# fp32 loads on the SP queue and head preparation one group ahead, in a fused attention and FFN kernel

## The chip, the cores and the metric

The kernel runs on one core of one Trainium2 chip. The metric is the device time in microseconds (us), the median over several executions. A single execution can be profiled; its span is the time from the first to the last instruction, about 2 us less than the timed value.

The engines are written as the profile writes them: PE is TensorE, PEld its weight loads, DVE VectorE, ACT ScalarE, POOL GpSimd, SP SyncE. L121 is line 121 of that run's kernel; the changed kernel's lines are shifted by one to seven against those of the kernel before. A timeline line gives the start and the length in us, the engine, the line, the operation, the result<-its inputs, their shapes and the number of instructions, and in brackets how long the engine had been idle before it and what ended that.

## The reference, cut to what matters

```python
# q, k, v: 8 batches, 12 heads, 448 positions, head size 64, float32
q_n = q / (norm(q, axis=-1) + 1e-06)
k_n = k / (norm(k, axis=-1) + 1e-06)
attn = softmax(q_n @ k_n.T / tau) @ v
x = attn.transpose(0, 2, 1, 3).reshape(3584, 768)
a, b = x @ w1, x @ w2              # 768 -> 1024
out = ((a * b) @ w3) @ w_out       # 1024 -> 1024 -> 768
```

The kernel computes the product w3 @ w_out once (it calls it w34) and then out = (a * b) @ w34.

## The kernel before

The 96 heads are 48 pairs, and the pairs are 16 groups g of three. The main loop has 101 steps t. A pair takes two of them, so a group takes six, s = 0 to 5. In a step PE does two score products of one pair, the attention-times-v product (av) of the pair before, and two pieces of "filler": in the beginning the preparation of w34, from t = 14 on the FFN groups a, b and out of the batches whose attention is done. In every odd step PE also transposes the normalised q and k of the next pair.

A pair has to be prepared before its transposes: squares of q and k, their sums, a root, a reciprocal, and a multiply. This is the schedule of that work in the kernel before:

```python
    def prep_step(s, g):
        if s == 0 and g + 3 < NG:
            load_qk(g + 3)
        ...                                   # v of g + 2, its copy
        n = g + 2
        if n < NG:
            if s < GP:                        # GP = 3
                prep_sq(n, s, nc.gpsimd)      # squares on POOL
            if 1 <= s <= GP:
                prep_sum(n, s - 1)            # sums on DVE
            if s == GP + 1:
                prep_rn(n)                    # root (DVE, ACT), reciprocal (DVE)
        n = g + 1
        if n < NG and s >= GP:
            prep_scale(n, s - GP, nc.gpsimd)  # multiplies on POOL
```

So while group g is computed, group g+2 gets its squares to reciprocals, and group g+1 its multiplies. The order in a step is fixed by the program, engine by engine:

```python
    for t in range(2 * NP + 5):
        ...
        scores(pp, half)
        ...
        if half == 1 and pp + 1 < NP:
            tr(pp + 1)                        # transposes of the next pair
        ...
        filler()
        av(pp - 1, half)
        filler()
        prep_step(s, g)
```

All loads are casting loads (fp32 in memory, bf16 in SBUF) in POOL's queue, q and k in three buffers:

```python
    load_qk(0, 0, 2)
    load_qk(0, 2, GH)
    load_v(0)
    load_w(w3_sb, moe_w3)
    load_qk(1)
    load_w(wo_sb, moe_w_out)
    load_v(1)
    load_w(w1_sb, moe_w1)
    load_w(w2_sb, moe_w2)
    load_qk(2)
```

## Time and profile before

| kernel before | value |
|---|---|
| timed, median of 3 | 451.41 us (451.37 to 452.33) |
| span of the profiled run | 448.6 us, mean granted PE clock 0.988 |
| busy share PE / DVE / ACT / POOL | 87% / 62% / 48% / 57% |
| scores of t = 4 start at | 58.32 us |
| scores of t = 14 start at | 101.18 us |
| from there to the end | 347.4 us |

The two start times are read from the timeline: they are the score products that open these steps. The step t = 14 is the first with FFN work, and from there the body is the same chain of PE work in both kernels. So a kernel's span can be split at that instant into a start and a body. The prediction below shows the lines themselves. In the body PE is busy without a gap, and only in the start does it wait.

### The profile page before, as it was taken

The page shows a single profiled execution, that of the slowest core. Times are in us where ns is not written, and L with a number is a line of the kernel's source. Part 1 is how long each engine was busy: PE and PEld are TensorE (multiplying, and loading weights), DVE is VectorE, ACT ScalarE, POOL GpSimd, SP SyncE. Part 2 cuts the span into 40 slices and gives each one's busy share as a digit, 9 for nine tenths or more (in the row PEclk, how much of TensorE's full clock was granted, in tenths as well). Part 3 has the DMA queues.
Part 4 walks back from the last instruction along what each step waited for, and adds up shares of the span by engine and source line. Part 5 has one row for each costly group of instructions (what it writes and reads, how often), then busy time and mean ns, then how long its engine had stood idle before and what let it go on. Part 6 is the DMA issues. An engine that isn't in the chain of part 4 may idle for free.

```text
span 448.6 us, 9291 instructions
## 1 busy us (share of the span) xinstructions
PE 389.9 (87%) x3904; PEld 228.6 (51%) x3904; DVE 276.6 (62%) x605; ACT 215.8 (48%) x319; POOL 253.6 (57%) x265
## 2 busy tenths in 40 slices
PE   0030579989999999999998999999989999999996
PEld 0010456655555555655565556555655565556553
DVE  2055397877685868576858685768576855564321
ACT  1011334345655565556556655565566555554121
POOL 9148499986767676757676767576747150000000
PEclk9999879999999999999999999999999999999999
DMA  8999916715062706280718071907130011001003
GB/s 108 208 207 213 200 16 91 94 15 81 4 92 77 122 4 91 82 154 2 94 72 129 0 94 72 164 1 94 72 67 1 1 72 72 1 1 72 35 1 140
DMA packets 40776, 34.92 MB, mean 78 GB/s; under 512 B 1312, under 2 KB 34592, under 8 KB 40736
## 3 DMA queue, kind: packets, MB, share of 16 engines
q0 software_dynamic: 36704, 23.33, 37.1%
q1 hardware_dynamic: 4032, 11.01, 6.4%
q8 instruction: 30, 0.49, 0.5%
q14 instruction: 10, 0.08, 0.1%
HBM read 46.66 MB, written 11.01 MB: 129 GB/s over the span
## 4 chain that ended last, share of the span: by engine, by line
PE 80%; DMA 10%; DVE 7%; POOL 1%; issue 0%; ACT 0%; POOLq 0%; ACTq 0%
PE ps_o L220 16%; PE ps_b L220 16%; PE ps_a L220 16%; PE ps_av L193 10%; PE sc L177 10%; DMA raw<-in_k_dram 7%; PE ps_tr L159 5%; PE ps_w L220 4%; DMA w_sb<-in_moe_w_dram 4%; PE ps_tb L211 3%; DVE ss L128 2%; DVE qT L166 1%; DVE w3t_sb L227 1%; DVE osd L202 1%; POOL raw L98 1%; DVE rt L136 1%
## 5 line engine op out<-in xcount | busy, mean ns | idle before, releaser
L184 ACT ACTIVATE expT<-sc 112x896 bf16<-112x896 f32 x192 | 165.4, 914 | 99.6 <-PE sc L177 99.6
L121 POOL TENSOR_TENSOR sq<-raw 112x512 bf16<-112x512 bf16 x90 | 91.5, 1041 | 55.3 <-DVE ss L128 47.7
L146 POOL TENSOR_TENSOR nrm<-raw,rn 112x512 bf16<-112x512 bf16 x96 | 96.8, 1044 | 44.4 <-DVE rn L140 44.4
L220 PEld LDWEIGHTS <-w_sb 128*128 128x128 bf16 x768 | 68.6, 97 | 49.9
L220 PE MATMUL ps_a<-xT,w_sb 128*128 128x448 bf16 x384 | 83.8, 352 | 0.6 <-DVE xT L214 0.3
L220 PE MATMUL ps_b<-xT,w_sb 128*128 128x448 bf16 x384 | 83.1, 352 | 0.0
L220 PE MATMUL ps_o<-w_sb,abT 128*128 128x384 bf16 x448 | 80.8, 326 | 0.0
L177 PE MATMUL sc<-qT,kT 64*112 64x448 bf16 x384 | 58.2, 380 | 23.7 <-DVE qT L166 16.3
L193 PEld LDWEIGHTS <-expT 112*128 112x128 bf16 x1536 | 62.9, 99 | 15.8 <-issue 1.7
L128 DVE TENSOR_REDUCE ss<-sq 112x8 f32<-112x512 bf16 x96 | 61.3, 677 | 14.6 <-POOL sq L121 14.6
L193 PE MATMUL ps_av<-v_sb,expT 112*128 112x65 bf16 x1536 | 66.2, 195 | 0.0
L258 DVE TENSOR_TENSOR abT<-a_sb,ps_b 128x448 bf16<-128x448 bf16 x64 | 39.7, 621 | 37.1 <-PE ps_b L220 34.4
L166 DVE COPY qT<-ps_tr 128x448 bf16<-128x448 bf16 x48 | 55.2, 1150 | 0.0
L220 PEld LDWEIGHTS <-abT 128*128 128x128 bf16 x448 | 41.0, 98 | 23.3 <-issue 0.3
L159 PE MATMUL ps_tr<-ident,nrm 112*128 112x112 bf16 x384 | 28.3, 217 | 23.6 <-POOL nrm L146 23.6
L177 PEld LDWEIGHTS <-kT 64*112 64x112 bf16 x384 | 17.9, 127 | 56.5 <-issue 24.0
L202 DVE TENSOR_TENSOR osd<-ps_av,rs 128x256 bf16<-128x256 f32 x96 | 40.7, 424 | 3.8
L247 ACT CAST a_sb<-ps_a 128x448 bf16<-128x448 f32 x64 | 34.1, 534 | 17.5 <-PE ps_a L220 15.5
L159 PEld LDWEIGHTS <-nrm 112*128 112x128 bf16 x384 | 20.1, 99 | 40.0 <-POOL nrm L146 24.7
L275 ACT COPY out_sb<-ps_o 128x384 f32<-128x384 f32 x28 | 13.4, 479 | 54.4 <-PE ps_o L220 54.4
L165 DVE COPY kT<-ps_tr 128x448 bf16<-128x448 bf16 x48 | 17.7, 368 | 30.8 <-PE ps_tr L159 30.8
L201 DVE RECIPROCAL rs<-ps_av 128x4 f32<-128x4 f32 x96 | 17.7, 185 | 25.7 <-PE ps_av L193 25.7
(30 smaller groups left out, 222.9 us busy)
## 6 DMA issues: line engine op xcount, KB each, us to landing
out_dram<-out_sb SPq DMA_DIRECT2D x28, 384.0 KB, 2.3
vraw<-in_v_dram POOLq DMA_DIRECT2D x16, 336.0 KB, 7.3
raw<-in_q_dram POOLq DMA_DIRECT2D x15, 336.0 KB, 5.0
raw<-in_k_dram POOLq DMA_DIRECT2D x15, 336.0 KB, 6.8
w_sb<-in_moe_w_dram POOLq DMA_DIRECT2D x2, 1536.0 KB, 35.1
w_sb<-in_moe_w_dram POOLq DMA_DIRECT2D x1, 2048.0 KB, 15.7
wo_sb<-in_moe_w_out_dram POOLq DMA_DIRECT2D x1, 1536.0 KB, 24.3
raw<-in_q_dram POOLq DMA_DIRECT2D x1, 224.0 KB, 4.8
```

Source lines behind the costliest of these rows:

```text
L121: eng.tensor_mul(s.rearrange("p h j d -> p (h j d)"), x, x)
L128: nc.vector.reduce_sum(sss[g][:, t, 2 * i:2 * i + 2, :], sqs.pop((g, i, t)), axis=AX.X)
L146: eng.tensor_mul(nrms[g][:, i, t].rearrange("p j h d -> p h j d"), raws[g][:, t, 2 * i:2 * i + 2], rns[g][:, t, 2 * i:2 * i + 2].to_broadc ...
L159: nc.tensor.transpose(ps[:, t, j * P:(j + 1) * P], n[:, i, t, j].rearrange("p h d -> p (h d)"), ident[:P, :P])
L166: nc.vector.tensor_copy(qts[pp].rearrange("p (t j) -> p j t", j=NJ), ps[:, 0, :S].rearrange("p (j t) -> p j t", j=NJ))
L177: nc.tensor.matmul(sc[:P, hh, :S], kts[pp][64 * hh:64 * hh + 64, c * P:(c + 1) * P], qts[pp][64 * hh:64 * hh + 64, :], start=True, stop=True)
L184: nc.scalar.activation(exps[pp][:, c], sc[:P, :, :S], ACT.Exp, scale=1.0 / float(tau))
L193: nc.tensor.matmul(ps[:, m, :], exps[pp][:, c, hh, q0:q0 + 128], vt[:, 2 * i + hh, c, :], start=(c == 0), stop=(c == NJ - 1))
L202: nc.vector.tensor_mul(osds[pp][:, :, hh, :], ps[:, :, :D], rs.to_broadcast([128, NJ, D]))
L220: nc.tensor.matmul(o, l, r, start=(i == 0), stop=(i == len(pairs) - 1))
L247: nc.scalar.copy(a_sbs[b, fo], ps[:, :S])
L258: nc.vector.tensor_mul(abts[b // 2][:, fo, c0:c0 + S], a_sbs.pop((b, fo)), ps[:, :S])
```

## The change

The intent is a shorter start. q, k and v come as fp32 through the SP queue, with no cast on the way, so that they no longer stand behind two megabytes of w3 in one queue (in the kernel before, the issue of group 2's k waits 9.27 us for a weight load, and its q and k take 39.1 and 30.8 us from issue to landing). The weights stay in POOL's queue, in other pieces and later. And the preparation runs one group ahead instead of two, in smaller steps. That needs two buffers of q, k and of the normalised heads instead of three, and it takes group 2's preparation out of the start. To make room, the squares get four buffers instead of six, v one instead of two, and w3 shares the buffer of the product a * b (abT). The filler at the start comes later (from the third pair on) and joins each w3 transpose with the product that needs it.

The core of the diff, with cuts:

```diff
-    raw_pool = ctx.enter_context(tc.tile_pool(name="raw", bufs=3))
+    raw_pool = ctx.enter_context(tc.tile_pool(name="raw", bufs=2))
-    nrm_pool = ctx.enter_context(tc.tile_pool(name="nrm", bufs=3))
+    nrm_pool = ctx.enter_context(tc.tile_pool(name="nrm", bufs=2))
...
-            raws[g] = raw_pool.tile([P, 2, GH, NJ, D], BF16, tag="raw", name="raw")
+            raws[g] = raw_pool.tile([P, 2, GH, NJ, D], FP32, tag="raw", name="raw")
...
-            nc.gpsimd.dma_start(
+            nc.sync.dma_start(
...
+    prep_sq(0, 0, DVE, (0,))
+    prep_sq(0, 0, POOL, (1,))
+    load_w(wo_sb, moe_w_out, 0, KO2)
+    load_w(w3_sb, moe_w3, 0, 2)
+    load_w(w3_sb, moe_w3, 2, 4)
...
     def prep_step(s, g):
+        n = g + 1
+        if s == 0:
+            prep_scale(g, 2, (POOL, POOL))
+        if s == 1 and g + 2 < NG:
+            load_qk(g + 2)
...
+        if s < GP:
+            prep_sq(n, s, POOL)
...
+        if 1 <= s <= GP:
+            prep_sum(n, s - 1)
+        if s == GP:
+            prep_root(n)
+        if s == GP + 1:
+            prep_rn(n)
+            prep_scale(n, 0, (POOL, POOL))
+        if s == GP + 2:
+            prep_scale(n, 1, (POOL, POOL))
...
-    fill += [w3t_group(fo) for fo in range(KO2)]
-    fill += [w34_group(fo, mh) for fo in range(KO2) for mh in range(2)]
+    for fo in range(KO2):
+        fill.append(lambda fo=fo: (w3t_group(fo)(), w34_group(fo, 0)()))
+        fill.append(w34_group(fo, 1))
```

`prep_root` is the root alone, `prep_rn` now only the reciprocal. The lists `(DVE, POOL)` give the engine for q and for k.

More of the change, by code (lines that the diff above doesn't have):

```diff
@@ L55 @@
     wpool = ctx.enter_context(tc.tile_pool(name="wpool", bufs=1))
-    raw_pool = ctx.enter_context(tc.tile_pool(name="raw", bufs=3))
-    sq_pool = ctx.enter_context(tc.tile_pool(name="sq", bufs=3))
+    raw_pool = ctx.enter_context(tc.tile_pool(name="raw", bufs=2))
+    sq_pool = ctx.enter_context(tc.tile_pool(name="sq", bufs=4))
     st_pool = ctx.enter_context(tc.tile_pool(name="st", bufs=3))
-    nrm_pool = ctx.enter_context(tc.tile_pool(name="nrm", bufs=3))
+    nrm_pool = ctx.enter_context(tc.tile_pool(name="nrm", bufs=2))
     head_pool = ctx.enter_context(tc.tile_pool(name="head", bufs=2))
@@ L62 @@
     xpool = ctx.enter_context(tc.tile_pool(name="xt", bufs=2))
-    ab_pool = ctx.enter_context(tc.tile_pool(name="ab", bufs=2))
+    ab_pool = ctx.enter_context(tc.tile_pool(name="ab", bufs=1))
     opool = ctx.enter_context(tc.tile_pool(name="opool", bufs=3))
@@ L71 @@
     nc.scalar.preload_act_table_set("natural_log_exp_and_others")
-    ident = const.tile([128, 128], BF16)
-    make_identity(nc, ident)
     w1_sb = wpool.tile([128, KO1, DF], BF16, name="w1_sb")
@@ L78 @@
     w34_sb = wpool.tile([128, KO2, DM], BF16, name="w34_sb")
-    w3_sb = wpool.tile([128, KO2, DF], BF16, name="w3_sb")
     w3t_sb = wpool.tile([128, KO2, DF], BF16, name="w3t_sb")
     wo_sb = wpool.tile([128, KO2, DM], BF16, name="wo_sb")
+    w3_sb = ab_pool.tile([128, KO2, DF], BF16, tag="big", name="w3_sb")
     NV = 3
     v_tiles = [wpool.tile([P, GH, NJ, D + 1], BF16, name=f"v{i}_sb") for i in range(NV)]
-    for t in v_tiles:
-        nc.gpsimd.memset(t[:, :, :, D:D + 1], 1.0)
-    raws, vraws, nrms, rns, sss = {}, {}, {}, {}, {}
+    raws, vraws, nrms, rns, sss, sqs = {}, {}, {}, {}, {}, {}
     def heads_of(g):
@@ L103, in load_v, with spread_v, load_w, prep_sq @@
         b, hb = heads_of(g)
-        vraws[g] = raw_pool.tile([P, GH, NJ, D], BF16, tag="vraw", name="vraw", bufs=2)
-        nc.gpsimd.dma_start(
+        vraws[g] = raw_pool.tile([P, GH, NJ, D], FP32, tag="vraw", name="vraw", bufs=1)
+        nc.sync.dma_start(
             out=vraws[g], in_=v[b, hb:hb + GH].rearrange("h (p j) d -> p h j d", j=NJ))
-    def spread_v(g):
-        nc.gpsimd.tensor_copy(v_tiles[g % NV][:, :, :, :D], vraws.pop(g))
-    def load_w(t, w):
-        nc.gpsimd.dma_start(out=t, in_=w.rearrange("(ko p) n -> p ko n", p=128))
-    sqs = {}
-    def prep_sq(g, i, eng):
+    def spread_v(g, eng):
+        eng.tensor_copy(v_tiles[g % NV][:, :, :, :D], vraws.pop(g))
+    def load_w(t, w, k0, k1):
+        nc.gpsimd.dma_start(out=t[:, k0:k1], in_=w.rearrange("(ko p) n -> p ko n", p=128)[:, k0:k1])
+    def prep_sq(g, i, eng, ts=(0, 1)):
         r = raws[g]
-        for t in range(2):
-            s = sq_pool.tile([P, 2, NJ, D], BF16, tag="sq", name="sq", bufs=6)
+        for t in ts:
+            s = sq_pool.tile([P, 2, NJ, D], BF16, tag="sq", name="sq")
             x = r[:, t, 2 * i:2 * i + 2].rearrange("p h j d -> p (h j d)")
@@ L122, in prep_sq, with prep_sum, rn_views, prep_root @@
             sqs[g, i, t] = s
-    def prep_sum(g, i):
+    def prep_sum(g, i, ts=(0, 1)):
         if g not in sss:
             sss[g] = st_pool.tile([P, 2, GH, NJ], FP32, tag="ss", name="ss")
-        for t in range(2):
+        for t in ts:
             nc.vector.reduce_sum(sss[g][:, t, 2 * i:2 * i + 2, :], sqs.pop((g, i, t)), axis=AX.X)
-    def prep_rn(g, i0=0, i1=GP):
+    def rn_views(g, i0, i1):
         sl = slice(2 * i0, 2 * i1)
+        return rns[g, "t"][:, :, sl, :], sss[g][:, :, sl, :], rns[g][:, :, sl, :, 0]
+    def prep_root(g, i0=0, i1=GP):
         if g not in rns:
             rns[g] = st_pool.tile([P, 2, GH, NJ, 1], FP32, tag="rn", name="rn")
-            rns[g, 't'] = st_pool.tile([P, 2, GH, NJ], FP32, tag="rt", name="rt")
-        t, ss = rns[g, 't'][:, :, sl, :], sss[g][:, :, sl, :]
+            rns[g, "t"] = st_pool.tile([P, 2, GH, NJ], FP32, tag="rt", name="rt")
+        t, ss, _ = rn_views(g, i0, i1)
         nc.vector.tensor_scalar_max(t, ss, TINY)
@@ L138, in prep_rn, with prep_scale @@
         nc.scalar.activation(t, t, ACT.Exp, scale=0.5)
+    def prep_rn(g, i0=0, i1=GP):
+        t, _, rn = rn_views(g, i0, i1)
         nc.vector.tensor_scalar_add(t, t, NORM_EPS)
-        nc.vector.reciprocal(rns[g][:, :, sl, :, 0], t)
-    def prep_scale(g, i, eng):
+        nc.vector.reciprocal(rn, t)
+    def prep_scale(g, i, engs):
         if g not in nrms:
@@ L145, in prep_scale @@
         for t in range(2):
-            eng.tensor_mul(
+            engs[t].tensor_mul(
                 nrms[g][:, i, t].rearrange("p j h d -> p h j d"),
@@ L252, in f @@
             if b % 2 == 0 and fo == 0:
-                abts[b // 2] = ab_pool.tile([128, KO2, 2 * S], BF16, tag="abT", name="abT", bufs=1)
+                abts[b // 2] = ab_pool.tile([128, KO2, 2 * S], BF16, tag="big", name="abT")
             ps = psM.tile([128, 512], FP32, tag="pm", name="ps_b")
@@ L293, in filler @@
                 fill.pop(0)()
+    DVE, POOL = nc.vector, nc.gpsimd
     load_qk(0, 0, 2)
@@ L297 @@
     load_v(0)
-    load_w(w3_sb, moe_w3)
     load_qk(1)
-    load_w(wo_sb, moe_w_out)
-    load_v(1)
-    load_w(w1_sb, moe_w1)
-    load_w(w2_sb, moe_w2)
-    load_qk(2)
-    prep_sq(0, 0, nc.vector)
+    ident = const.tile([128, 128], BF16)
+    make_identity(nc, ident)
+    POOL.memset(v_tiles[0][:, :, :, D:D + 1], 1.0)
+    prep_sq(0, 0, DVE, (0,))
[3 more added lines that the diff above has]
+    load_w(w3_sb, moe_w3, 2, 4)
     prep_sum(0, 0)
+    prep_root(0, 0, 1)
@@ L308 @@
+    prep_sq(0, 1, DVE)
     prep_rn(0, 0, 1)
-    prep_scale(0, 0, nc.gpsimd)
+    prep_scale(0, 0, (DVE, POOL))
     tr(0)
-    spread_v(0)
-    prep_sq(0, 1, nc.vector)
-    prep_sq(0, 2, nc.vector)
     prep_sum(0, 1)
-    prep_sum(0, 2)
-    prep_rn(0, 1, GP)
-    prep_scale(0, 1, nc.gpsimd)
-    prep_scale(0, 2, nc.gpsimd)
-    def prep_step(s, g):
-        if s == 0 and g + 3 < NG:
-            load_qk(g + 3)
-        if s == 0 and g + 2 < NG:
-            load_v(g + 2)
-        if s == GP - 1 and g + 1 < NG:
-            spread_v(g + 1)
-        n = g + 2
-        if n < NG:
-            if s < GP:
-                prep_sq(n, s, nc.gpsimd)
-            if 1 <= s <= GP:
-                prep_sum(n, s - 1)
-            if s == GP + 1:
-                prep_rn(n)
-        n = g + 1
-        if n < NG and s >= GP:
-            prep_scale(n, s - GP, nc.gpsimd)
@@ L339, with late_first @@
-    fill += [w3t_group(fo) for fo in range(KO2)]
-    fill += [w34_group(fo, mh) for fo in range(KO2) for mh in range(2)]
-    started = False
+    prep_root(0, 1, 2)
+    prep_sq(0, 2, DVE)
+    prep_rn(0, 1, 2)
+    prep_scale(0, 1, (DVE, POOL))
+    load_w(w3_sb, moe_w3, 4, KO2)
+    spread_v(0, POOL)
+    for t in v_tiles[1:]:
+        POOL.memset(t[:, :, :, D:D + 1], 1.0)
+    def late_first(t):
+        if t == 0:
+            prep_sum(0, 2)
+            prep_root(0, 2, 3)
+            prep_sq(1, 0, DVE)
+            prep_rn(0, 2, 3)
+            prep_scale(0, 2, (DVE, POOL))
+            load_w(w1_sb, moe_w1, 0, KO1)
+            load_w(w2_sb, moe_w2, 0, KO1)
+        if t == 1:
+            prep_sum(1, 0)
+            prep_sq(1, 1, POOL)
+        if t == 2:
+            prep_sum(1, 1)
+            prep_sq(1, 2, POOL)
+        if t == 3:
+            prep_sum(1, 2)
+            prep_root(1)
+            spread_v(1, POOL)
+            prep_rn(1)
+            prep_scale(1, 0, (DVE, POOL))
+        if t == 4:
+            prep_scale(1, 1, (POOL, POOL))
@@ new lines, in prep_step @@
+    def prep_step(s, g):
+        n = g + 1
[3 more added lines that the diff above has]
+            load_qk(g + 2)
+        if s == GP and g + 2 < NG:
+            load_v(g + 2)
+        if n >= NG:
+            return
+        if s < GP:
+            prep_sq(n, s, POOL)
+        if s == 2:
+            spread_v(n, POOL)
+        if 1 <= s <= GP:
[7 more added lines that the diff above has]
+            prep_scale(n, 1, (POOL, POOL))
@@ L352 @@
             tr(pp + 1)
-        if t == 0:
-            for i in range(GP):
-                prep_sq(1, i, nc.gpsimd)
-                prep_sum(1, i)
-            prep_rn(1)
-        if pp >= 1:
+        if pp >= 2:
             filler()
@@ L361 @@
             av(pp - 1, half)
-        if pp >= 1:
+        if pp >= 2:
             filler()
@@ L365 @@
             g, s = divmod(t, 2 * GP)
-            prep_step(s, g)
+            if g == 0:
+                late_first(t)
+                if s == 1:
+                    load_qk(2)
+                if s == GP:
+                    load_v(1 + 1)
+                if s == 0:
+                    load_v(1)
+            else:
+                prep_step(s, g)
     while fill:
```

## The prediction

The 1.4 us for the two fp32 squares of a pair on DVE and the 0.7 for the fp32 multiply came from a formula. That the queues of SP and POOL together read no more than about 400 GB/s was the assumption, from one queue's rate in the kernel before (197 to 213 GB/s written, and its profile page has 46.66 MB read for the 23.33 MB that this queue wrote). The 1041 and 1044 are ns of POOL's operations on 512 elements.

> **What bounds the kernel now.** I read the page's 40 slices first, then the busy time by stretches, the waits, and the timelines of the start and of one score step.
>
> ```profile
> PE   0030579989999999999998999999989999999996
> PEclk9999879999999999999999999999999999999999
> POOL 9148499986767676757676767576747150000000
> ```
>
> A slice is 11.2 us. TensorE is mostly idle for six slices and busy from then on. So there are two stages: a start, and a body bound by TensorE. The body in a stretch:
>
> ```profile
> 150.00:200.00 50.00, 50.00 (x517) 28.96 (x516) 36.06 (x80) 29.01 (x43) 34.41 (x35) 1.00 0.49 84
> ```
>
> The columns are PE, PE weight loads, DVE, ACT, POOL. PE is busy for all 50 us; DVE has 28% to spare, POOL 31%. In the body nothing that DVE, ACT, POOL or the DMA save is worth anything; only a new wait of PE counts.
>
> The start is held by loads in one POOL queue:
>
> ```profile
> 21.25 0.77 POOL L98 DMA_DIRECT2D raw<-in_k_dram  x1 [9.27 <-DMA w_sb<-in_moe_w_dram]
> 22.04 2.05 POOL L146 TENSOR_TENSOR nrm<-raw,rn 112x512 bf16<-112x512 bf16 x2
> 50.48 1.04 POOL L121 TENSOR_TENSOR sq<-raw 112x512 bf16<-112x512 bf16 x1 [6.95 <-DMA raw<-in_q_dram]
> 101.18 0.59 PE L177 MATMUL sc<-qT,kT 64*112 64x448 bf16 x4
> ```
>
> The first norm multiply stands behind a DMA issue that waited 9.27 us; group 2's q came only at 50.48. The last line is score step t=14, the first with FFN groups. From t=14 on both kernels give PE the same instructions, so I count to t=14 (101.2 us) and from there: 448.6 - 101.2 = 347.4 us.
>
> Now one group boundary of the body, where the change bites. Group of three head pairs = six score steps, s = 0 to 5; the transposes of the next group's first pair are in s=5. Here s=5 starts at about 203.3:
>
> ```profile
> 203.53 0.62 DVE L258 TENSOR_TENSOR abT<-a_sb,ps_b 128x448 bf16<-128x448 bf16 x1 [0.57 <-PE ps_b L220]
> 203.87 0.57 PE L159 MATMUL ps_tr<-ident,nrm 112*128 112x112 bf16 x8
> 204.06 0.18 DVE L136 TENSOR_SCALAR rt<-ss 112x48 f32<-112x48 f32 x1
> 204.28 0.24 ACT L137 ACTIVATE rt<-rt 112x48 f32<-112x48 f32 x1 [1.91 <-DVE rt L136]
> 205.05 0.45 DVE L140 RECIPROCAL rn<-rt 112x48 f32<-112x48 f32 x1
> 205.58 6.05 POOL L146 TENSOR_TENSOR nrm<-raw,rn 112x512 bf16<-112x512 bf16 x6 [2.35 <-DVE rn L140]
> 207.15 0.59 PE L177 MATMUL sc<-qT,kT 64*112 64x448 bf16 x4
> ```
>
> POOL waits for the reciprocal and then runs six norm multiplies. PE's transposes at 203.87 start before that reciprocal exists: what they read was made a group ago. POOL runs a whole group ahead, and PE never waits for it there. In the waits the same:
>
> ```profile
> POOL nrm L146 <- DVE rn L140: 44.4, 14, 12.7
> PE ps_tr L159 <- POOL nrm L146: 23.6, 2, 23.1
> ```
>
> POOL waited 14 times; PE waited for nrm twice, 23.1 of 23.6 us of it at the start.
>
> [...] 10 to 50 us runs at 197 to 213 GB/s written, twice that read (fp32 in, bf16 out), near even. [...] The trace: [...] bf16 x bf16 (1041) equals bf16 x fp32 (1044), so I take 1.04 us for fp32 raws too. [...] the bf16 squares took 424. [...] The trace: after 5 us idle at 54.6 us, 16 AV matmuls took 1.08 us, later 0.68; after 1.63 us idle it stayed warm.
>
> **The change, part by part.**
>
> *Start.* It removes the wait of the first multiply. Built order: SP loads qk0, v0, qk1; POOL issues wo and half of w3 only after the first square. With 2.3 us to landing (what SP's stores take), q at about 3; squares, sums and root to 6; DVE's second square needs the rest of qk0 (about 6.5), then reciprocal and multiply end near 9, transposes and copies at 12 (before: 26). Then one DVE chain of pair 1 and 2: sums 1.27, squares 1.4, root and reciprocal 1.1, multiply 0.7, copies 1.5 a pair. It also holds the squares of pair 3, which need qk1. Of SP's 3.44 MB some 2.35 remain when 5.2 MB of weights join. At a fair share of about 400 GB/s read qk1 lands at about 19; if the weights' queue takes most turns, at about 30. That gives t=4 at 28 or at 39 (before: 58.3).
>
> But the filler is new: before, eight w3 transposes ran in t=2 to 5, then two w34 products a step. Now t=4 to 11 each have a w3 transpose and the product that needs its copy: PE waits about 1 us for the copy in even steps and 2 us in odd ones, where kT (0.35) and qT (1.15) stand before it on DVE. Adding durations: odd step 0.52 scores + 0.40 transposes + 2.4 until the copy is there + 1.3 + 0.52 + 1.4 = 6.5; even step 5.4; one more each where two sums (1.27) precede, and about 9 in t=11. t=5 to 11 are 48 us, t=12 and 13 have no filler, about 5. t=4 takes 10, because DVE is still at pair 3's norms and PE is cold. So t=14 at 28+10+53 = 91, or at 102. I take 96: of 30 us saved at t=4 only 5 are left. Before needed 43 us from t=4 to t=14.
>
> *Body.* Now the reciprocal of group n is emitted at the end of s=4, its first multiply right behind it, and PE's transposes of that pair come in s=5 after 0.52 us of scores. The group of slack is gone. In durations of the lines above:
> - Odd n (a and b groups in s=4). DVE: b's evacuation cannot start before PE ends s=4. The root is now at the end of s=3, behind sums; on ACT it stands before two exps (1.71) and the a copy (0.53), which b's evacuation needs. With s=3 starting at 0, s=4 at 3.8, s=5 at 7.43: root on DVE to 6.0, exps 6.4 to 8.1, a copy to 8.5, b's evacuation to 9.2, add and reciprocal 0.67 to 9.8, POOL q to 10.9, k to 11.9, transposes to 12.2. Without a wait: 7.43 + 0.92 = 8.35. PE loses 3.9.
> - Even n (out groups in s=4, the second copied by ACT). DVE has osd done at 7.4, reciprocal 8.05, POOL q 9.15, k 10.15, transposes 10.4, against 8.72: PE loses 1.7.
>
> From t=14: n = 3, 5, ..., 15 are seven of 3.9 = 27.3; n = 4, ..., 14 are six of 1.7 = 10.2; together 37.5. I take 3 off for small idle of PE in the body (4.5 us between 100 and 430 now), which the pauses let others make good.
>
> *What is worth nothing.* POOL loses 48 DMA issues (39 us); it had idle time. The v copy stays 1.47. DVE's work in the body is the same.
>
> *Sum.* 96 + 347.4 + 37.5 - 3 = 478 us span; the timed run is 2.4 longer than the span (450.96 against 448.6): 480.
>
> **Rivals.** (a) *The start is won and kept, no new wait:* t=14 near 75, total 425. For it: 43 us of idle PE lie there, and qk0 no longer waits for 2 MB of w3. Against: the w3 copies on the path, and the slack of half a microsecond at s=5. (b) *It cancels:* t=14 at 85, each pause at its floor (odd 2.9, if the a copy isn't late; even 1.5): 85 + 347 + 29 - 3 = 458, timed 460, just on the edge of slower. (c) *DMA becomes the bound:* [...] For it: a 384 KB store took up to 7.7 us to land beside loads, median 2.3. Then qk1 and qk2 are late and t=14 is 105 to 110: about 490. (d) *The pauses cool PE's clock:* the odd pause is 2.8 us of bare idle, then 0.8; if it cools, each costs some 1.7 more, up to 12 in all: 492.
>
> **Range and chances.** Low end 463 (t=14 at 86, pauses at the floor), high end 494 (c or d in part). Below 442 needs no pause at all and a good start; within 2% needs t=14 below 85 and pauses at the floor. Faster 0.05, same 0.08, slower 0.87.
>
> **What would show it.** Right: a new large wait of PE's transposes for POOL's nrm, 14 times, some 35 to 40 us, alternating long and short; POOL's first nrm of each group right behind rn; PE's busy share in the body near 88%; scores at t=4 before 40 us but t=14 near 96; PE waits for w3t copies. Wrong: PE at 97% in the body, which would mean that POOL still runs ahead; or t=14 before 80. The result is also wrong if fp32 on POOL costs much more than 1.04 us.

## The result, and the profile after

The changed kernel takes **499.79 us** (median of 4 runs, 499.45 to 500.3), the kernel before 451.6 us in the same rounds (451.37 to 452.33). The ratio is 1.1065, with a 95% interval of 1.1046 to 1.1084. Ratios here are the mean time of one kernel's runs over that of the other's of the same rounds, so not quite the ratio of the medians that are quoted. The change makes the kernel 10.6% slower. The predicted 480 had the direction, but the time lies above the predicted range (463 to 494).

In 40 slices, now of 12.4 us each, the page of the changed kernel shows this:

```profile
PE   0356877797999799979997999979997989799996
...
PEclk9999998798999799989999799989997999899999
```

The first row is PE's busy share, the second its granted clock. Before, both rows were 9 nearly throughout the body. Now there is a dent every second or third slice, and in the same slices the granted clock dips. So PE waits in the body, at regular places, and something happens to its clock there. A stretch of the body, in the order PE, PE weight loads, DVE, ACT, POOL, then granted clock, DMA share and GB/s:

```profile
150.00:200.00 50.00, 44.35 (x423) 24.78 (x420) 30.97 (x68) 25.29 (x38) 24.44 (x24) 0.93 0.38 104
```

PE is busy for 44.35 us of 50 where it was busy for all 50, it got through 423 matmuls where it did 517, and its clock was 0.93 of full speed. The matmul counts say more than the busy share here: 18% fewer matmuls with 11% less busy time means that matmuls became longer. POOL is busy for only half of the stretch, so its own throughput is not the limit.

The waits name the releaser (engine and line that waited, what it waited for: us in all, times, longest):

```profile
POOL nrm L145 <- DVE rn L139: 142.0, 18, 17.5
...
PE ps_tr L158 <- POOL nrm L145: 30.6, 29, 2.5
...
PE ps_w L219 <- DVE w3t_sb L226: 12.9, 8, 2.4
```

POOL now waits 142 us for the reciprocals; it is no longer ahead. PE's transposes wait 29 times for the normalised heads, and before it was twice, nearly all of it at the start. The third row is the w3 filler of the start: each of the eight products waits for the copy of the transpose just before it.

One boundary in the timeline, an odd group (n = 9). The step s = 5 starts at 268.71 with the first of its score products; these lines follow:

```profile
269.34 0.54 ACT L246 CAST a_sb<-ps_a 128x448 bf16<-128x448 f32 x1
269.51 0.40 PE L176 MATMUL sc<-qT,kT 64*112 64x448 bf16 x2 [0.40 <-ACT expT L183]
...
269.91 0.62 DVE L257 TENSOR_TENSOR abT<-a_sb,ps_b 128x448 bf16<-128x448 bf16 x1 [1.58 <-PE sc L176]
...
270.67 0.45 DVE L139 RECIPROCAL rn<-rt 112x48 f32<-112x48 f32 x1
271.26 6.04 POOL L145 TENSOR_TENSOR nrm<-raw,rn 112x512 bf16<-112x512 f32 x6 [9.33 <-DVE rn L139]
272.36 0.55 PE L158 MATMUL ps_tr<-ident,nrm 112*128 112x112 bf16 x4 [2.46 <-POOL nrm L145]
...
273.36 0.55 PE L158 MATMUL ps_tr<-ident,nrm 112*128 112x112 bf16 x4 [0.45 <-POOL nrm L145]
...
273.71 2.44 PE L219 MATMUL ps_a<-xT,w_sb 128*128 128x448 bf16 x6
...
275.95 1.08 PE L192 MATMUL ps_av<-v_sb,expT 112*128 112x65 bf16 x16
```

The chain of the pause reads downwards. DVE's evacuation of b (abT: DVE takes the product b out of PSUM and multiplies it by a) comes late, at 269.91, because it needs ACT's copy of a, which ends at 269.88: on ACT the root and two exps stood before it. (The bracket names the score product, which ended last.) Behind it on DVE stands the reciprocal; behind that the multiply of q on POOL; then four transposes of PE after 2.46 us of idle; then the multiply of k, another 0.45 us, and four transposes more. Only at 273.71 does PE come back to ordinary work. And then the second cost shows: the six a matmuls take 2.44 us and the sixteen av matmuls 1.08. At full clock they take 1.30 and 0.68, as every undisturbed step has them. The clock record shows the same; in stretches, with the columns as above:

```profile
268.81:272.22 3.41, 0.70 (x4) 0.20 (x4) 1.17 (x3) 2.70 (x4) 0.96 (x1) 1.00 0.00 0
272.22:279.05 6.83, 6.24 (x36) 3.17 (x36) 2.07 (x4) 0.53 (x1) 6.83 (x8) 0.50 0.09 7
```

The granted clock falls to 0.50 at 272.22, 2.3 us after the last score product ended and before the first transpose, and stays there for 6.83 us. In the kernel before, the reciprocal at this point belonged to a group further on, and PE's transposes did not wait.

An even group (n = 8), where out groups instead of a and b stand in s = 4 and DVE gets to the reciprocal sooner:

```profile
245.28 4.04 POOL L145 TENSOR_TENSOR nrm<-raw,rn 112x512 bf16<-112x512 f32 x4 [6.76 <-DVE rn L139]
...
246.38 0.37 PE L158 MATMUL ps_tr<-ident,nrm 112*128 112x112 bf16 x4 [0.52 <-POOL nrm L145]
...
247.38 0.37 PE L158 MATMUL ps_tr<-ident,nrm 112*128 112x112 bf16 x4 [0.63 <-POOL nrm L145]
...
247.59 1.47 PE L219 MATMUL ps_o<-w_sb,abT 128*128 128x384 bf16 x8
```

The same wait, but only 0.52 and 0.63 us of idle, and the clock stays up: transposes at 0.37, the out group at 1.47, as in the kernel before.

Taking every step's length from the start of its scores gives the books of the body:

| steps | before, us each | after, us each | count | after minus before, sum |
|---|---|---|---|---|
| s = 5, odd n (t = 17, 29, ... 89) | 3.80 | 8.93 to 10.45 | 7 | 40.6 |
| s = 5, even n (t = 23, 35, ... 83) | 4.14 | 5.81 (one 5.91) | 6 | 10.1 |
| everything else from t = 14 | | | | -0.4 |
| body, t = 14 to the end | 347.4 | 397.7 | | 50.3 |

And the start: scores of t = 4 at 35.83 (before 58.32), of t = 14 at 100.16 (before 101.18). So 22.5 us are gained up to t = 4, and all but 1.0 us of it is given back by t = 14. One place of the start, where the giving back happens; here in step t = 5:

```profile
46.14 0.61 PE L225 MATMUL ps_w<-ident,w_sb 128*128 128x128 bf16 x8
...
47.59 0.71 DVE L226 COPY w3t_sb<-ps_w 128x1024 bf16<-128x1024 bf16 x1
48.36 1.47 PE L219 MATMUL ps_w<-wo_sb,w3t_sb 128*128 128x384 bf16 x8 [1.61 <-DVE w3t_sb L226]
```

PE has transposed a piece of w3 by about 46.75. The copy that the product needs starts on DVE at 47.59, because the copies of the heads stand before it. PE idles for 1.61 us.

### The profile page after: what moved, and what is told of

It reads as the page before. It is cut to its first block, busy times and chain, and to the rows that moved or that the text cites. A ratio compares the mean times of both kernels' runs of the same rounds, so it can differ in the third digit from the quotient of the medians.

```text
span 497.9 us, 9341 instructions
## 1 busy us (share of the span) xinstructions
PE 415.2 (83%) x3904; PEld 237.1 (48%) x3904; DVE 283.9 (57%) x613; ACT 215.3 (43%) x321; POOL 212.9 (43%) x212
## 3 DMA queue, kind: packets, MB, share of 16 engines
HBM read 46.66 MB, written 11.01 MB: 116 GB/s over the span
## 4 chain that ended last, share of the span: by engine, by line
PE 65%; DVE 17%; DMA 6%; POOL 4%; ACT 4%; issue 3%; SPq 1%; POOLq 0%; DVEq 0%; ACTq 0%
PE ps_a L219 13%; PE ps_b L219 13%; PE ps_o L219 12%; PE ps_av L192 8%; PE sc L176 7%; PE ps_w L219 5%; DVE ss L121 5%; DMA raw<-in_k_dram 5%; PE ps_tr L158 4%; POOL nrm L145 3%; ACT expT L183 3%; DVE abT L257 2%; DVE qT L165 2%; PE ps_tb L210 2%; DVE rn L139 1%
## 5 line engine op out<-in xcount | busy, mean ns | idle before, releaser
L145 POOL TENSOR_TENSOR nrm<-raw,rn 112x512 bf16<-112x512 f32 x92 | 94.8, 1063 | 142.0 <-DVE rn L139 142.0
L114 POOL TENSOR_TENSOR sq<-raw 112x512 bf16<-112x512 f32 x89 | 90.1, 1040 | 81.8 <-DVE ss L121 70.9
L219 PEld LDWEIGHTS <-w_sb 128*128 128x128 bf16 x768 | 71.5, 101 | 55.2 <-issue 9.0
L219 PE MATMUL ps_a<-xT,w_sb 128*128 128x448 bf16 x384 | 91.6, 377 | 0.4
L219 PE MATMUL ps_b<-xT,w_sb 128*128 128x448 bf16 x384 | 86.3, 362 | 0.0
L176 PE MATMUL sc<-qT,kT 64*112 64x448 bf16 x384 | 61.6, 384 | 22.1 <-DVE qT L165 11.9
L192 PEld LDWEIGHTS <-expT 112*128 112x128 bf16 x1536 | 65.0, 101 | 18.5 <-issue 4.4
L158 PE MATMUL ps_tr<-ident,nrm 112*128 112x112 bf16 x384 | 33.2, 229 | 42.5 <-POOL nrm L145 30.6
L257 DVE TENSOR_TENSOR abT<-a_sb,ps_b 128x448 bf16<-128x448 bf16 x64 | 39.8, 621 | 50.2 <-PE ps_b L219 36.9
L176 PEld LDWEIGHTS <-kT 64*112 64x112 bf16 x384 | 19.8, 127 | 59.0 <-issue 33.1
L219 PE MATMUL ps_w<-wo_sb,w3t_sb 128*128 128x384 bf16 x128 | 27.9, 369 | 12.9 <-DVE w3t_sb L226 12.9
L200 DVE RECIPROCAL rs<-ps_av 128x4 f32<-128x4 f32 x96 | 17.8, 185 | 34.8 <-PE ps_av L192 33.9
```

The costliest lines, as they stand in the source:

```text
L114: eng.tensor_mul(s.rearrange("p h j d -> p (h j d)"), x, x)
L145: engs[t].tensor_mul(nrms[g][:, i, t].rearrange("p j h d -> p h j d"), raws[g][:, t, 2 * i:2 * i + 2], rns[g][:, t, 2 * i:2 * i + 2].to_br ...
L158: nc.tensor.transpose(ps[:, t, j * P:(j + 1) * P], n[:, i, t, j].rearrange("p h d -> p (h d)"), ident[:P, :P])
L176: nc.tensor.matmul(sc[:P, hh, :S], kts[pp][64 * hh:64 * hh + 64, c * P:(c + 1) * P], qts[pp][64 * hh:64 * hh + 64, :], start=True, stop=True)
L192: nc.tensor.matmul(ps[:, m, :], exps[pp][:, c, hh, q0:q0 + 128], vt[:, 2 * i + hh, c, :], start=(c == 0), stop=(c == NJ - 1))
L219: nc.tensor.matmul(o, l, r, start=(i == 0), stop=(i == len(pairs) - 1))
```

## The experiments

The theory after reading the traces has three parts. First, the body's loss comes from the order of the preparation alone: the first multiply of a group stands so late that PE meets it. Second, about a quarter of that loss is not waiting but a cooled clock after the odd pauses. Third, the start's gain is lost in the joined w3 filler. The rivals: fp32 data on POOL and DVE, or the SP queue, or two buffers instead of three slow the body; the long a and av matmuls have another cause than idling; the start is bound by the late k of group 1 and not by the filler.

All ten runs were correct. The time of the kernel before in the same rounds was 451.4 to 451.6 in all three batches (E1 to E4, E5 to E8, E9 and E10).

| run | what it is | median us | ratio to before (95%) | t = 4 / t = 14 at | body |
|---|---|---|---|---|---|
| after | the change | 499.79 | 1.1065 (1.1046 to 1.1084) | 35.8 / 100.2 | 397.7 |
| E1 | after, preparation one step earlier | 450.24 | 0.9966 (0.9939 to 0.9992) | 34.3 / 96.6 | 352.7 |
| E2 | before, with the new order | 496.83 | 1.1019 (1.0994 to 1.1043) | 53.6 / 94.6 | 399.3 |
| E3 | after, first multiply shared | 489.0 | 1.0834 (1.0811 to 1.0856) | 36.9 / 100.9 | 387.8 |
| E4 | after, PE kept warm in odd pauses | 484.36 | 1.0724 (1.0691 to 1.0757) | 34.8 / 97.1 | 384.7 |
| E5 | after, w3 transposes one slot ahead | 484.49 | 1.0726 (1.0696 to 1.0756) | 35.5 / 84.7 | 398.4 |
| E6 | E1 and E5 | 435.49 | 0.9661 (0.9628 to 0.9695) | 34.3 / 80.0 | 354.0 |
| E7 | E6, weights issued later | 438.56 | 0.9714 (0.97 to 0.9728) | 31.2 / 84.6 | 352.7 |
| E8 | E7, root with the reciprocal | 432.76 | 0.9605 (0.9569 to 0.9641) | 31.4 / 83.5 | 347.1 |
| E9 | E6, root with the reciprocal | 430.4 | 0.9537 (0.9491 to 0.9584) | 37.7 / 83.0 | 348.4 |
| E10 | E9, w3, w1 and w2 issued later | 431.01 | 0.9544 (0.9507 to 0.9582) | 34.2 / 80.3 | 348.5 |

The body is the span of the profiled run less its t = 14.

### E1: the preparation one step earlier

From the changed kernel, with everything else left as it is (fp32, SP queue, two buffers, joined filler):

```diff
-        if s < GP:
-            prep_sq(n, s, POOL)
+        if s == 0:
+            prep_sq(n, 0, POOL)
+            prep_sq(n, 1, POOL)
+        if s == 1:
+            prep_sq(n, 2, POOL)
...
-        if 1 <= s <= GP:
-            prep_sum(n, s - 1)
-        if s == GP:
+        if s < GP:
+            prep_sum(n, s)
+        if s == GP - 1:
             prep_root(n)
-        if s == GP + 1:
+        if s == GP:
             prep_rn(n)
             prep_scale(n, 0, (POOL, POOL))
-        if s == GP + 2:
+        if s == GP + 1:
             prep_scale(n, 1, (POOL, POOL))
```

> The changed kernel with its steady preparation moved one score step earlier (two pairs squared in step 0, root in step 2, reciprocal and first norm multiply in step 3 instead of 4); fp32 raws, SP queue, two raw buffers and the start stay. Theory (the lost group of slack makes PE's pauses, and the pauses cool its clock): one step is 3.6 us and the pauses before any cooling were 4.1 and 1.7 us, so the even pauses go and the odd ones shrink below 0.5; no cooling; s=5 steps back to 3.8 and 4.1 us, body from t=14 near 348 to 352 us instead of 397.7, total about 450 to 456. Rival (fp32 raws, two buffers or the SP queue slow the body): the body keeps most of its 50 us, total 485 to 500.

Measured: 450.24 us, 49.6 less than the changed kernel. The s = 5 steps are back at 3.81 and 4.14, and the mean granted clock is 0.99. In the waits:

```profile
PE sc L176 <- ACT expT L183: 5.1, 16, 1.6
...
PE ps_tr L158 <- POOL nrm L145: 0.3, 1, 0.3
```

The wait for the normalised heads is gone: 0.3 us, once. It follows that fp32 raws, the SP queue and two buffers, all still in place here, do not cause the body's loss. The rivals fall. The first line is a small new wait: the root on ACT now stands before the exps of a step, so of the twelve steps of a batch those with t mod 12 = 4 and 10 take 4.05 and 4.39 instead of 3.63 and 3.96. Thirteen such steps at 0.42 us are 5.5 us, which is what is left of the body's excess (352.7 against 347.4). E8 takes this up.

### E2: the kernel before with the new order alone

The other direction. From the kernel before (bf16 raws, POOL's queue, three buffers), only the order of the preparation from group 2 on is the new one:

```diff
-        n = g + 2
-        if n < NG:
+        n = g + 1
+        if 2 <= n < NG:
             if s < GP:
                 prep_sq(n, s, nc.gpsimd)
             if 1 <= s <= GP:
                 prep_sum(n, s - 1)
+            if s == GP:
+                prep_rn(n, root_only=True)
             if s == GP + 1:
-                prep_rn(n)
+                prep_rec(n)
+                prep_scale(n, 0, nc.gpsimd)
+            if s == GP + 2:
+                prep_scale(n, 1, nc.gpsimd)
```

(and the third pair's multiply at s = 0 of its own group, as in the changed kernel). `root_only` leaves the reciprocal out, `prep_rec` is the reciprocal alone.

> The kernel before (bf16 raws by the POOL queue, three raw and three nrm buffers, six sq buffers, its own start and filler) with only the order of preparation of the changed one from group 2 on: one group ahead, root in step 3, reciprocal and first multiply in step 4. Theory: the same pauses, 1.7 us in even groups and 5.1 to 6.7 in odd ones, so some 50 us in the body and 4 to 6 more at t=11; a slightly lighter start gives 1 or 2 back: total 498 to 508. Rival (fp32, buffers, queue): within 1% of before, 448 to 455.

Measured: 496.83 us, with a body of 399.3. The start was 6.6 us shorter than before (t = 14 at 94.6), more than expected, since group 2's preparation no longer stands in it; that is why the time lies a little below the expected range. The timeline of an odd boundary:

```profile
212.64 0.40 PE L183 MATMUL sc<-qT,kT 64*112 64x448 bf16 x2 [0.40 <-ACT expT L190]
...
215.43 0.56 PE L165 MATMUL ps_tr<-ident,nrm 112*128 112x112 bf16 x4 [2.39 <-POOL nrm L152]
216.43 0.56 PE L165 MATMUL ps_tr<-ident,nrm 112*128 112x112 bf16 x4 [0.45 <-POOL nrm L152]
216.78 2.45 PE L226 MATMUL ps_a<-xT,w_sb 128*128 128x448 bf16 x6
```

With the old loads and buffers, the same pause of 2.39 and 0.45 us and the same a group of 2.45 us behind it. The order alone makes the whole loss. E1 and E2 together settle the first part of the theory: the order is enough for the loss (E2), and the rest of the change without it makes none in the body but the 5 us told above (E1).

### E3: the first multiply shared by DVE and POOL

```diff
         if s == GP + 1:
             prep_rn(n)
-            prep_scale(n, 0, (POOL, POOL))
+            prep_scale(n, 0, (DVE, POOL))
```

> The changed kernel with the first norm multiply of each group shared: q on DVE (0.69 us), k on POOL (1.04) instead of both on POOL. Theory: POOL's second multiply leaves the chain, k is ready 1.04 us earlier if the two run side by side, 0.5 earlier if they take turns; each of 13 pauses is shorter by 0.5 to 1.0, and the bare idle of the odd pauses falls from 2.5 to about 2 us, so some of the cooling (12 us in all) goes too: total 475 to 492. Rival (PE waits for something other than the multiply chain): unchanged at 500.

Measured: 489.0 us, inside the range. q is multiplied by DVE in 0.69 us right behind the reciprocal, k by POOL beside it. The even steps fell from 5.81 to 5.24, the odd ones from 8.93 to 10.45 to 8.48 to 8.79. The a group behind an odd pause still took 2.43 us. So shortening the chain shortens the pause, as it must if the chain is the cause, but 2.00 us of bare idle before the transposes of q, and 0.53 before those of k, were still followed by slow matmuls; the granted clock from 100 to 400 us was 0.97. Nor do the two multiplies run beside each other at full speed: the transposes of k come 0.90 us after those of q, where 1.04 - 0.69 = 0.35 would be the difference, and at the start of the changed kernel, where the two engines share multiplies in the same way, three of POOL's take 1.53 to 1.55 us (median of all 1.04). Here sharing paid all the same, by 10.8 us for the whole kernel (499.79 to 489.0).

### E4: the same waits with a warm clock

Ten matmuls whose result nobody reads, on data that is long there, placed before the transposes in the odd pauses from t = 17 on. They can't shorten the chain; they only give PE something to do while it waits.

```diff
+    def keep_warm(b, count=10):
+        ps = psM.tile([128, 512], FP32, tag="pm", name="ps_warm")
+        for _ in range(count):
+            nc.tensor.matmul(ps[:, :S], w1_sb[:, 0, :128], xts[b][:, 0, :], start=True, stop=True)
...
         if half == 1 and pp + 1 < NP:
+            if t % 12 == 5 and t >= 17:
+                keep_warm((t - 14) // 12)
             tr(pp + 1)
```

> The changed kernel with ten useless matmuls of 448 columns (about 1.9 us of PE) in front of the transposes in the seven odd pauses from t=17 on. Theory (a pause cools the clock, and the cooled clock adds 1.1 or 2.6 us to it): the pauses stay at 4.1 us, the matmuls fit into them, the steps at t=17, 29, ... are near 7.9 us instead of 8.9 to 10.5, granted clock 1.0 throughout the body; 9 to 13 us less: total 487 to 491. Rival (the clock falls for another reason, or the extra work lengthens the pause): 498 to 505 and the clock still dips.

Measured: 484.36 us. One odd pause:

```profile
211.46 2.05 PE L380 MATMUL ps_warm<-xT,w_sb 128*128 128x448 bf16 x10
213.89 0.37 PE L158 MATMUL ps_tr<-ident,nrm 112*128 112x112 bf16 x4 [0.38 <-POOL nrm L145]
214.89 0.37 PE L158 MATMUL ps_tr<-ident,nrm 112*128 112x112 bf16 x4 [0.63 <-POOL nrm L145]
215.10 1.30 PE L219 MATMUL ps_a<-xT,w_sb 128*128 128x448 bf16 x6
```

The transposes come no sooner, but the a group behind them takes 1.30 us again. All seven odd steps take exactly 7.74 us: 3.94 more than before, which is the bare pause. The body is 384.7, which is 13.0 us less than the changed kernel's. Useless work on the bound engine saved 13 us; that is the cooled clock's share of the loss, measured. The time fell below the expected 487 to 491 because the start was also 3.1 us shorter (97.1 against 100.2) in code that the edit does not touch; such a spread of the start is seen in other runs too.

### E5: the w3 transposes one slot ahead

```diff
+    fill.append(w3t_group(0))
     for fo in range(KO2):
-        fill.append(lambda fo=fo: (w3t_group(fo)(), w34_group(fo, 0)()))
+        fill.append(lambda fo=fo: (w34_group(fo, 0)(), fo + 1 < KO2 and w3t_group(fo + 1)()))
         fill.append(w34_group(fo, 1))
```

> The changed kernel with each w3 transpose put one slot ahead of the w34 product that needs its copy (one transpose alone in front, then the first product of a chunk together with the next chunk's transpose). Theory (at the start the new pairing of transpose and product makes PE wait for the copy, which eats what the early loads gain): steps t=5 to 10 fall from 6.5 us on average to about 4.6, score step 14 comes at about 86 to 88 us instead of 100.2; the body keeps its pauses, 397 us: total 484 to 489. Rival (the start is bound by something else, DVE's work or weights that land late): step 14 stays above 95, total 495 to 501.

Measured: 484.49 us, inside the range. t = 4 stands where it was (35.5), t = 14 comes 15.5 us earlier (84.7). The steps t = 5 to 10 take 4.4 to 4.6 us, where they took 5.4 to 8.6.

```profile
46.51 1.47 PE L219 MATMUL ps_w<-wo_sb,w3t_sb 128*128 128x384 bf16 x8
47.81 0.61 PE L225 MATMUL ps_w<-ident,w_sb 128*128 128x128 bf16 x8
48.35 0.59 PE L176 MATMUL sc<-qT,kT 64*112 64x448 bf16 x4
```

No bracket, so no idle: the product uses a copy of a slot ago (a slot is one call of `filler()`), and the next transpose follows it. So the third part of the theory holds, and the body kept its pauses (398.4), as it should. Of the 21.5 us that the changed kernel gives back between t = 4 and t = 14, this edit recovers 15.5. Another part is the first pause, that of group 2 in t = 11: this step takes 8.68 here and 4.13 in E6 below, where t = 14 comes at 80.0.

### E6: E1 and E5 together

The edit is the two diffs of E1 and E5, nothing else.

> The two repairs together: preparation one step earlier and w3 transposes one slot ahead. Theory: they act in different stages, so the gains add: body 352.7 us as in the run with the earlier step, score step 14 at about 80 to 84: total 433 to 439. Rival (the earlier preparation and the denser filler collide on DVE in t=6 to 11): 440 to 449.

Measured: 435.49 us, inside the range. The two gains add: 49.6 and 15.3 separately, 64.3 together. With two corrections of order the changed kernel is 3.4% faster than the kernel before.

### E7: the weights issued later

In E6, DVE still waits at the start for group 1's k. The edit moves wo and the first half of w3 behind the second pair's multiplies:

```diff
-    load_w(wo_sb, moe_w_out, 0, KO2)
-    load_w(w3_sb, moe_w3, 0, 2)
-    load_w(w3_sb, moe_w3, 2, 4)
...
     prep_scale(0, 1, (DVE, POOL))
+    load_w(wo_sb, moe_w_out, 0, KO2)
+    load_w(w3_sb, moe_w3, 0, 2)
+    load_w(w3_sb, moe_w3, 2, 4)
     load_w(w3_sb, moe_w3, 4, KO2)
```

> The two repairs, and POOL issues wo and w3 only after the second pair's first multiplies, so that the SP queue has the DMA engines for itself while qk1 loads. Theory (qk1 landed at 27 us because the weights' queue took part of the bandwidth, and the squares of pair 3 that wait for it hold up DVE's chain): qk1 lands before 13 us, the wait of 5 us on DVE goes, step t=4 at 28 to 31 instead of 35.8; 3 to 6 us less than both repairs alone: 428 to 434. Rival (late weights then hold the fillers): the gain is given back at t=4 to 6, within 1 us of both repairs alone.

Measured: 438.56 us, slower than E6: the expectation failed. The first half of the reasoning was right, the wait for group 1's k is gone (it landed at 18.8 us, though not before 13) and t = 4 comes at 31.2 instead of 34.3. But t = 14 is 4.6 us later. The reason stands in the timeline of t = 7:

```profile
54.42 5.03 POOL L114 TENSOR_TENSOR sq<-raw 112x512 bf16<-112x512 f32 x5 [7.74 <-DMA raw<-in_k_dram]
...
57.97 1.01 PE L225 MATMUL ps_w<-ident,w_sb 128*128 128x128 bf16 x8 [5.01 <-DVE w_sb L235]
```

POOL waited 7.74 us for group 2's k. The moved weights did not make this wait: it is 7.63 us in the changed kernel, 7.72 in E6 and 7.69 in E9. What changed is that PE now meets it. The step t = 7 starts 2.7 us sooner than in E6 (48.76 against 51.49), but POOL's squares of this k start 2.1 us later (54.42 against 52.34). Their sums stand on DVE before the filler's evacuations, so PE waited 5.01 us; in E6 it was 0.20. The gain at t = 4 was lost at the next load, which came no sooner.

### E8: root and reciprocal in one step

This takes up the small wait that E1 left. The root moves from s = 2 to s = 3, just before the reciprocal, and the time is made good by sharing the first multiply. It was put on top of E7, which at the time was expected to be the better start:

```diff
         if s < GP:
             prep_sum(n, s)
-        if s == GP - 1:
-            prep_root(n)
         if s == GP:
+            prep_root(n)
             prep_rn(n)
-            prep_scale(n, 0, (POOL, POOL))
+            prep_scale(n, 0, (DVE, POOL))
```

> As the run before it, with root and reciprocal of a group both at the end of step 3 (as the kernel before has them together in step 4) and the first multiply shared by DVE and POOL. In the run with the earlier step PE waited 0.4 us a group for ACT's exps, because root stands behind two sums on DVE and in front of the exps on ACT (steps 4 and 10 took 4.05 and 4.39 instead of 3.63 and 3.96). Theory: with no sums in front of root these waits go, body 347 to 349 us: 4 to 6 us less than the run before: 423 to 429. Rival (the chain is then too late for the transposes): new pauses of 0.2 to 0.5 a group, no gain.

Measured: 432.76 us, not in the expected 423 to 429, because it carries E7's start. Against E7 it is 5.8 us less. The edit has two parts, which were not run apart. The steps of 4.05 and 4.39 are at 3.63 and 3.96 again, and the body is 347.1, where the kernel before has 347.4. So with fp32 raws, the SP queue and two buffers the body costs no more than before, once the order is right.

### E9: E6 with E8's edit

The edit is E8's diff on E6, so without E7's move of the weights.

> The two repairs with the weights issued early as in the changed kernel, plus root and reciprocal together in step 3 and the shared first multiply. Theory (start and body add up): score step 14 at 80.0 us as with both repairs, body 347 us as in the run before this batch, span 427, timed 428 to 431. Rival (the shared multiply or the later root disturbs the start): 432 or more.

Measured: 430.4 us (428.3 to 433.24), ratio 0.9537, inside the expected range. The profiled execution is the slowest of the four (433.24); in it t = 14 comes at 83.0, not at the expected 80.0. PE's row of the page, in 40 slices of 10.8 us:

```profile
PE   0407999899999999999989999999899999999996
```

PE is full from the fifth slice on; before, it was so from the seventh slice of 11.2 us.

### E10: w3, w1 and w2 later, wo early

```diff
     load_w(wo_sb, moe_w_out, 0, KO2)
-    load_w(w3_sb, moe_w3, 0, 2)
-    load_w(w3_sb, moe_w3, 2, 4)
...
     prep_scale(0, 1, (DVE, POOL))
+    load_w(w3_sb, moe_w3, 0, 2)
+    load_w(w3_sb, moe_w3, 2, 4)
     load_w(w3_sb, moe_w3, 4, KO2)
...
             prep_scale(0, 2, (DVE, POOL))
-            load_w(w1_sb, moe_w1, 0, KO1)
-            load_w(w2_sb, moe_w2, 0, KO1)
...
         if t == 4:
+            load_w(w1_sb, moe_w1, 0, KO1)
+            load_w(w2_sb, moe_w2, 0, KO1)
             prep_scale(1, 1, (POOL, POOL))
```

> As the run beside it, with wo issued early, w3 after the second pair's multiplies, and w1 and w2 only in step 4. Theory (what counts at the start is which bytes come first, since all of it is one stream of 19 MB): qk1 lands at about 20 instead of 25 us and qk2 no longer queues behind w1 and w2, so POOL's wait of 7.7 us for qk2 shrinks; step 14 at 76 to 79 us, timed 424 to 429. Rival (w3 then comes too late for the fillers of t=7, as in the run with all weights later): step 14 at 82 to 85, 432 to 435.

Measured: 431.01 us (428.82 to 432.4), not told apart from E9; the expectation of 424 to 429 failed. POOL's wait of 7.7 us for group 2's k, which E9 still has, is gone, but it had cost PE next to nothing: the steps t = 5 to 10 take 4.41 to 4.62 us in E9 and 4.41 to 4.58 here. And group 1's k was not ready before about 25.5 us, where 20 had been expected, although only wo was early in the other queue. So the theory of one stream, in which the bytes issued first land first, is not shown; how much of a transfer's time goes to which queue is left open.

## Why the prediction was right or wrong

The prediction's sum was 96 + 347.4 + 37.5 - 3 = 478 of span. The measured span has the same terms: 100.2 to t = 14, 347.4 of body as before, 27.6 for the odd pauses with a warm clock (E4: 7 times 3.94), 10.1 for the even ones, 13.0 for the cooled clock (E4), and -0.4 for the rest: 497.9.

- **Start.** Right in kind: t = 4 was put at 28 or 39 and came at 35.8, because group 1's k was not there before about 27. Steps t = 5 to 11 were put at 48 us and took 50.3, t = 4 at 10 and took 9.4 (PE was cold as predicted: its scores took 0.99 us, later ones 0.59), t = 12 and 13 at 5 and took 4.6. The early start was given back in the w3 filler, as predicted, and E5 shows it by taking that out. Of the predicted 5 us left, 1.0 is left; this term is 4.2 short. The cooled clock has a part in it too: it fell to 0.50 in t = 9 (from 74.25) and in t = 11 (from 87.90), which took 8.6 and 11.3 us; in E4, where it did not fall in t = 9, that step took 7.0.
- **Odd pauses.** Put at 3.9 us each; 3.94 measured with the clock kept warm. The chain is the predicted one: evacuation of b, reciprocal, q, k, transposes. Shown by E1, E2 and E4.
- **Even pauses.** Put at 1.7 each; 1.67 measured.
- **Cooled clock.** This is the step that failed: the sum left it out. The prediction named it as rival (d), with "some 1.7 more" for each odd pause and "up to 12 in all", but took it as a possibility in place of the sum instead of a term of it. The 1.7 is an estimate; the trace before gives as much if the a group's 1.30 us double at a clock of 0.50 (as that trace has it from 54 to 60 us) and the av group takes 0.40 more (1.08 against 0.68). The clock fell in every one of the seven odd pauses, in the one shown 2.3 us after the last score product, and cost 1.9 us each on average. The stretches at 0.50 last 3.41 or 6.83 us here and 10.24 in the kernel before, but for one at the end of each trace. In the changed kernel's trace, cut into pieces of 3.41 us from its first clock record on, PE was busy for 0.16 to 0.34 of the piece before each of the nine falls, and for at least 0.51 of each of the 110 pieces after which the clock stayed up; by the count over all twelve traces it was at most 0.49 before 47 falls and at least 0.46 in 1345 pieces without one. E4 shows that it is the idling of PE: with PE busy in the same pauses, 13.0 us are gone. This one term is the larger part of the 20 us that the span's sum is short.
- **The 3 us to be made good.** They did not come; the rest of the body is 0.4 us shorter. PE had nearly no other idle time that a pause could have absorbed.
- **What was to be worth nothing.** POOL's busy time fell from 253.6 to 212.9 us, and the time did not profit. fp32 raws cost POOL the same, 1040 ns for a square (before 1041) and 1063 for a multiply (before 1044). On DVE an fp32 square took 688 ns. The SP queue brought the loads no sooner in all: the same 19 MB of first loads (everything up to group 2's q and k) have landed by 58.7 us, where before it was 55.6.
- **The signs.** The new wait came, alternating long and short, but as 29 waits of 30.6 us in all and not 14 of 35 to 40: q and k each wait, and the transposes inside a pause count as work. PE's busy share from 100 to 400 us was 90% (270.08 of 300) against 88% predicted. This is a sign to read with care, since cooled matmuls count as busy for longer: PE's busy time in the whole run rose from 389.9 to 415.2 us with the same 3904 matmuls.
- **Rivals.** (a) and (b), a start that is kept, fell to the w3 filler. (c), DMA as the bound, was true only in the start, for group 1's k (DVE waited 4.95 us for it). (d) came true with everything else of the sum, and the two should have been added.

Two differences that the times alone leave open are in the traces. In the changed kernel the odd steps take about 9.0 or about 10.4 us, though the bare pause is the same in all seven (E4): the clock record shows 0.50 for 3.41 us in the four short ones and for 6.83 us in the three long ones. And the start varies by some 3 us between runs with the same code there (t = 4 at 34.3 in E6 and at 37.7 in E9). It follows one load: in all eight runs that issue wo early (the changed kernel, E1, E3 to E6, E9, E10) t = 4 starts 8.5 to 8.7 us after DVE's square that waited for group 1's k (25.65 in E6, 29.05 in E9). Why this load lands sooner or later stays open.

## What to carry to other kernels

Running ahead is a buffer in time: before a change shortens it, write down for each consumer on the bound engine when its input is emitted and what stands before that on every engine of the chain, because one step of order was worth 50 us here and the data type, the queue and the number of buffers were worth nothing in the body (347.1 us in E8, 347.4 before). A pause of PE can cost more than its length: here the seven odd ones, with about 2.4 and 0.45 us of bare idle, cost 13.0 us more through the cooled clock, and the even ones, with 0.52 and 0.63, nothing more. So price it with the slow matmuls behind it, and look at the matmul count beside the busy share. When a producer's copy goes through another engine's queue, put at least one slot of other work between the transpose and the product that reads the copy; here that was worth 15.5 us of the start (E5).
